# Decoding the first float64 weights through PSUM, with the rebias multiply on ScalarE

## The chip, the cores and the metric

The kernel runs on one core of a Trainium2 chip. TensorE (PE) multiplies matrices into PSUM, VectorE (DVE) and ScalarE (ACT) read PSUM and work elementwise, GpSimd (POOL) works elementwise on SBUF, and SyncE (SP) issues most DMAs. The five engines run their own instruction lists in order and wait for each other by semaphores. The metric is the device time of one execution in microseconds (us), less is better.

## The reference

The weights come as float64, everything else as float32. For each of 8 batches and 8 heads (576 tokens of 64 values), linear attention:

```python
q_s = exp(q - max(q, -1)); q_s /= sum(q_s, -1) + 1e-9
k_s = exp(k - max(k, tokens)); k_s /= sum(k_s, tokens) + 1e-9
attn = q_s @ (k_s.T @ v)
```

The heads, side by side, are x of 576 x 512 per batch. Then a token mixer with a residual, and two channel MLPs, the second after a layer norm:

```python
u = x + (relu(x.T @ w_tok1) @ w_tok2).T
y = u + relu(u @ w_ch1) @ w_ch2
out = y + relu(norm(y) * g_ln @ w2_ch1) @ w2_ch2
```

## The kernel before, in words

Products are made nearly exact in float32 by splitting each factor into a high part (rounded to TensorE's fp32r) and a low rest, and adding three products (high x high, high x low, low x high).

A weight arrives as pairs of 32-bit words. `decode` turns a chunk (up to 128 rows x 512 numbers) in a staging buffer into the high and low part in five steps:

1. rebias (L104): the upper word, read as a float32, is multiplied by 2^-112 in place;
2. shift (L107): that word is shifted left by 3 and masked, into a buffer `t`;
3. sign (L111): the sign bit is put into `t`;
4. low (L114): the top bits of the lower word are put in; the result goes back over the lower word in the staging buffer (for the weights of the second MLP it stays in `t`);
5. parts: the high part by a copy on ScalarE (L122), the low part by a subtraction on GpSimd (L123). The weights of the second MLP do this otherwise and are not in the part that is changed.

Steps 1 to 4 run on VectorE. `t` lies in SBUF, in two buffers. The staging buffers are six for the first weights (`st` two, `stages` two, `more` two).

The first weights are 30 chunks: six of the token mixer, then 24 of `w_ch1` and `w_ch2`. The class `Loads` decodes them in pairs. Its list for a pair is: both rebias steps, the parts of the pair before, the loads ahead, then both shifts, both signs, both lows. `pump(n)` issues the next n entries of the list.

The program is written out by a clock of ticks. In the first stage the attention units 0 to 7 (two heads each, batches 0 and 1; they are "early") begin four ticks apart, each with sixteen steps at set ticks, and after each tick the loop pumps four, later two, entries of the decoding. The steps of a unit that are named below: maximum of k (`kmx`, L398) and of q (`qm`, L404); transpose of `kmx` on TensorE into `pt` and its maximum `kmd` (L412); `kmd` spread out by TensorE into `pb`, copied by ScalarE into `kb` (L427); subtractions on GpSimd (L416, L431); exponentials on ScalarE (of q L441, of k into `kt` L444); sum of q (`qs`, L448) and scaling; `pk` = k x v (L463), whose sum column gives `ks` (L469); `pg` = q x w_tok1 (L486), copied into `gs` (L491); transposes of q into `pq` (L512), copied by L516; `ph` (L525), split into `hs` (L126 on ScalarE, L127 on VectorE); and twice `pu` (L540), split into `u` and `ue` (high by L122 on ScalarE, low by L123 on VectorE).

The eight PSUM banks are `acc0` to `acc3`, two `h` and two `a`. The early units take a bank for each of these products in turn from all eight (`psum(name, True)`); each product then waits until the bank's former content has been read.

After that stage the first MLP runs batch by batch (`Phase1`: L602 into `ph`, relu and split by L126 and L127, L619 into `acc`), with the rest of the 24 chunks decoded beside its first batch, and the units 8 to 31 beside the next ones. Then come the ends of the batches, the layer norm and the second MLP (`Phase2`: L732, L747).

Of the kernel before, what the change touches and what calls it, by code (L numbers as in the profile page):

```python
# [8 lines left out]
F32 = mybir.dt.float32  # L9
F32R = mybir.dt.float32r  # L10
U32 = mybir.dt.uint32
AF = mybir.ActivationFunctionType
ALU = mybir.AluOpType
# [3 lines left out]
P = 128  # L17
# [3 lines left out]
REBIAS = 2.0 ** -112  # L21
# [3 lines left out]
def kernel(  # L25
# [22 lines left out]
    nc = tc.nc  # L48
# [23 lines left out]
    main = ctx.enter_context(tc.tile_pool(name="main", bufs=1))  # L72
    ps_acc = ctx.enter_context(tc.tile_pool(name="ps_acc", bufs=1, space=PSUM))
    ps_hid = ctx.enter_context(tc.tile_pool(name="ps_hid", bufs=2, space=PSUM))
# [10 lines left out]
    def decode(st, w, hi, lo):  # L85


        rows, n = st.shape[0], st.shape[1]
        w0, w1 = st[:, :, 0], st[:, :, 1]
        wf = w1.bitcast(F32)  # L90
        t = main.tile([P, 512], U32, tag="t", bufs=2, name="t")[:rows, 0:n]

        o = t if w2p else w0
        x, vec = w(o.bitcast(F32)), nc.vector

        def parts():
            if w2p:
                vec.tensor_copy(out=hi, in_=x)  # L98
                nc.gpsimd.tensor_tensor(out=lo, in0=x, in1=hi.bitcast(F32), op=ALU.subtract)  # L99
            else:  # L100
                split(x, hi, lo, nc.gpsimd)

        return [
            lambda: vec.tensor_scalar(  # L104
                out=wf, in0=wf, scalar1=REBIAS, scalar2=None, op0=ALU.mult
            ),
            lambda: vec.tensor_scalar(  # L107
                out=t, in0=w1, scalar1=3, scalar2=0x7FFFFFF8,
                op0=ALU.logical_shift_left, op1=ALU.bitwise_and,
            ),  # L110
            lambda: vec.scalar_tensor_tensor(  # L111
                out=t, in0=w1, scalar=0x80000000, in1=t, op0=ALU.bitwise_and, op1=ALU.bitwise_or
            ),
            lambda: vec.scalar_tensor_tensor(  # L114
                out=o, in0=w0, scalar=29, in1=t,
                op0=ALU.logical_shift_right, op1=ALU.bitwise_or,
            ),
            parts,
        ]

    def split(x, hi, lo, engine):
        nc.scalar.activation(out=hi, in_=x, func=AF.Copy)  # L122
        engine.tensor_tensor(out=lo, in0=x, in1=hi.bitcast(F32), op=ALU.subtract)  # L123
# [7 lines left out]
    extra, bufs = [], []  # L131
# [9 lines left out]
    def ch1_chunk(dst, src, g, i, pool):  # L141
        def load():
            if dst is wa and (g, i) == (NF1 // 2 - 1, 0):

                extra[:] = [x for x in extra if x < 2]
            st = stage(512)
            a = src[2 * i * P:2 * (i + 1) * P, 4 * g * P:4 * (g + 1) * P]
            nc.sync.dma_start(
                out=st.rearrange("p (k f) t -> p k (f t)", k=2),
                in_=a.rearrange("(k p) f -> p k f", p=P),  # L150
            )
            return st

        def use(st):
            if i == 0:
                dst[g] = pool.tile([P, 2, KD, 2 * P], F32R, tag="w", bufs=pool_bufs[pool], name="w")
            w, kk = dst[g], slice(2 * i, 2 * i + 2)
            return decode(
                st, lambda x: x.rearrange("p (k f) -> p k f", k=2), w[:, 0, kk], w[:, 1, kk]
            )  # L160

        return load, use

    def ch2_chunk(dst, src, g, i, pool):
        def load():
            st = stage(512)
            f0 = (2 * g + i) * P
            nc.sync.dma_start(out=st.rearrange("p d t -> p (d t)"), in_=src[f0:f0 + P, :])
            return st

        def use(st):
            if i == 0:
                dst[g] = pool.tile([P, 2, 2, DM], F32R, tag="w", bufs=pool_bufs[pool], name="w")
            return decode(st, lambda x: x, dst[g][:, 0, i], dst[g][:, 1, i])

        return load, use
# [7 lines left out]
    w2p = []  # L184
# [3 lines left out]
    w1 = att.tile([P, 2, NC + 1, T], F32R, name="w1")  # L188
# [5 lines left out]
    def tok1_chunk(c0, n, rows):  # L194
        def load():
            st = stage(n * T)[:rows]
            if c0 < NC:
                src = w_tok1[0:S0].rearrange("(p c) t -> p c t", c=NC)[:, c0:c0 + n]
            else:
                src = w_tok1[S0:S].rearrange("(p c) t -> p c t", c=1)  # L200
            nc.sync.dma_start(out=st.rearrange("p (c t) w -> p c (t w)", c=n), in_=src)
            return st

        def use(st):
            return decode(
                st, lambda x: x.rearrange("p (c t) -> p c t", c=n),
                w1[:rows, 0, c0:c0 + n], w1[:rows, 1, c0:c0 + n],
            )

        return load, use  # L210
# [98 lines left out]
    rows = [P] * NC + [R]  # L309
# [51 lines left out]
    turns = [0]  # L361

    def psum(name, early=False):
        if early:
            turns[0] += 1
            i = turns[0] % 8
            if i < 4:
                return ps_acc.tile([P, 512], F32, tag=f"acc{i}", name=name)
            if i < 6:
                return ps_hid.tile([P, 512], F32, tag="h", name=name)  # L370
        return ps_att.tile([P, 512], F32, tag="a", name=name)

    class Unit:
# [34 lines left out]
        def k_top(self):  # L408
            pt = psum("pt", self.early)
            nc.tensor.transpose(out=pt[:, 0:P], in_=self.kmx, identity=ident)  # L410
            self.kmd = att.tile([P, 1], F32, tag="kmd", bufs=2, name="kmd")
            nc.vector.tensor_reduce(out=self.kmd, in_=pt[:, 0:P], axis=AX, op=ALU.max)  # L412
# [8 lines left out]
        def k_sub(self):  # L421
            pb = psum("pb", self.early)
            nc.tensor.transpose(
                out=pb[:, 0:P], in_=self.kmd.to_broadcast([P, P]), identity=ident
            )
            kb = place(self.n, "kb")
            nc.scalar.activation(  # L427
                out=kb[:, 0], in_=pb[:, 0:P].rearrange("p (h d) -> p h d", h=2), func=AF.Copy
            )
            self.kt = place(self.n, "kt")  # L430
            nc.gpsimd.tensor_tensor(  # L431
                out=self.kt, in0=self.kr.rearrange("p h c d -> p c h d"),
                in1=kb.to_broadcast([P, NC + 1, 2, D]), op=ALU.subtract,
            )
            if self.n + 3 < EARLY:
                load_qk(self.n + 3)
            elif self.n + 1 >= EARLY:
                load_qk(self.n + 1)
# [21 lines left out]
        def kv(self):  # L460
            pk = psum("pk", self.early)
            for c in range(NC + 1):
                nc.tensor.matmul(  # L463
                    out=pk[:, 0:2 * D + 2], lhsT=self.kt[:, c], rhs=vt[:, c, :],
                    start=(c == 0), stop=(c == NC),
                )
            load_v(self.n + 1)
            ks = att.tile([P, 1], F32, tag="ks", bufs=2, name="ks")
            nc.vector.tensor_scalar(  # L469
                out=ks, in0=pk[:, 2 * D:2 * D + 1], scalar1=1e-9, scalar2=None, op0=ALU.add  # L470
            )
            nc.vector.reciprocal(out=ks, in_=ks)
            for h in range(2):
                r = slice(h * D, (h + 1) * D)
                nc.vector.tensor_scalar(
                    out=self.kvn[r, r], in0=pk[r, r], scalar1=ks[r], scalar2=None, op0=ALU.mult
                )
            self.kvs = place(self.n, "kvs")
            split(self.kvn, self.kvs[:, 0], self.kvs[:, 1], nc.vector)
# [284 lines left out]
    with tc.manual_schedule():  # L764
# [5 lines left out]
        for x in spare[0:2]:  # L770
            x = x[:, 0:2 * W].rearrange("p (a h c d) -> p a h c d", a=2, h=2, d=D)
# [43 lines left out]
        for j in range(NB):  # L815
            o = Phase1(j)
            steps += [(o, f) for f in range(NF1)]
        for j in range(NB):
            o = Phase2(j)
# [21 lines left out]
        for o, f in steps:  # L841
# [32 lines left out]
            ps, n = o.L1(f, tick)  # L874
            h = main.tile([P, 2, 512], F32R, tag="h", bufs=LAG + 1, name="h")
# [42 lines left out]
```

## Time and profile before

| | us |
|---|---|
| median of three runs | 1720.69 |
| lowest, highest | 1718.91, 1722.46 |
| the profiled execution | 1719.21 |
| its span from first to last instruction | 1717.2 |
| PE, DVE, ACT, POOL busy over the span | 1654.5, 703.9, 376.8, 316.0 |

The busy shares are means over stages of different kinds. In the line of 40 slices of the profile TensorE is at 3, 6 and 8 tenths in the first three slices (43 us each) and at 9 in nearly all that follow, while VectorE is at 8 to 9 in the first three and at 2 to 4 in most others. A timeline row below gives the start, the duration, the engine, the line, the operation, what it writes and reads, and in brackets the idle time of the engine before it with what ended that.

### The profile page before, as it was taken

The numbers are of one execution on the slowest core, as the hardware profiler recorded it, in microseconds if no ns is written. First come the engines' busy times: TensorE is split into PE (matmuls) and PEld (weight loads), VectorE is DVE, ScalarE is ACT, GpSimd is POOL, SyncE is SP. The second block draws the span as 40 slices with busy tenths as digits, with TensorE's granted clock in tenths as the row PEclk, the third lists the DMA queues.
The fourth block names the chain that finished last, engine by engine and source line by source line (L and its number), as shares of the span: only waits on it lengthen the run. The fifth ranks groups of instructions, "written<-read, shape, count | busy, mean of one in ns | idle before, by whom it ended". The sixth has DMA issues, their size and how long they took to land.

```text
span 1717.2 us, 19988 instructions
## 1 busy us (share of the span) xinstructions
PE 1654.5 (96%) x8104; PEld 1383.7 (81%) x8104; DVE 703.9 (41%) x1342; ACT 376.8 (22%) x758; POOL 316.0 (18%) x213
## 2 busy tenths in 40 slices
PE   3689999999999999999999899999999999999999
PEld 3678888888888888888878688888888888888887
DVE  8987444334343444436267922131312122222211
ACT  3442232323233332321111111110111111111110
POOL 5553322223132332212113200000000000000000
PEclk9889999999999999999999999999999999999999
DMA  7442111212121211214123410101010101010010
GB/s 207 123 134 85 46 56 35 67 37 70 35 67 42 60 48 40 61 44 160 47 90 114 157 60 25 49 25 49 10 65 1 74 1 56 18 43 32 1 50 25
DMA packets 96763, 103.27 MB, mean 60 GB/s; under 512 B 60128, under 2 KB 76768, under 8 KB 93216
## 3 DMA queue, kind: packets, MB, share of 16 engines
q1 hardware_dynamic: 90272, 84.17, 16.5%
q10 hardware_dynamic: 5248, 9.44, 1.5%
q0 software_dynamic: 1152, 8.39, 1.2%
q8 instruction: 64, 1.05, 0.3%
q14 instruction: 27, 0.22, 0.0%
HBM read 81.00 MB, written 20.97 MB: 59 GB/s over the span
## 4 chain that ended last, share of the span: by engine, by line
PE 56%; DVE 3%; DMA 1%; POOL 0%; issue 0%; ACT 0%; SPq 0%; ACTq 0%; DVEq 0%
PE ph L732 22%; PE acc L747 22%; PE acc L619 5%; PE ph L602 5%; PE px L707 1%; PE pu L540 1%; DMA st<-in_moe_w_ch 0%; DVE t L111 0%; PE py L564 0%; PE pg L486 0%; POOL yT L633 0%; DVE st L671 0%; DMA y_dram<-yn 0%; DMA y<-y_dram 0%; DVE t L114 0%; DVE y L696 0%
## 5 line engine op out<-in xcount | busy, mean ns | idle before, releaser
L127 DVE SCALAR_TENSOR_TENSOR h<-ph,h 128x512 fp32r<-128x512 f32 x252 | 174.0, 691 | 685.9 <-ACT h L126 685.9
L732 PE MATMUL ph<-xT,w 128*128 128x512 f32 x1728 | 421.0, 392 | 3.5 <-DVE h L127 2.4
L747 PE MATMUL acc<-w,h 128*128 128x512 f32 x1728 | 420.0, 392 | 0.0
L732 PEld LDWEIGHTS ph<-xT,w 128*128 128x128 f32 x1728 | 322.8, 188 | 75.3 <-DVE h L127 3.2
L747 PEld LDWEIGHTS acc<-w,h 128*128 128x128 f32 x1728 | 323.0, 188 | 68.8
L126 ACT ACTIVATE h<-ph 128x512 fp32r<-128x512 f32 x252 | 150.6, 598 | 880.1 <-PE ph L732 645.7
L619 PE MATMUL acc<-h,w 128*128 128x512 f32 x1296 | 328.5, 396 | 0.0
L602 PE MATMUL ph<-u,w 128*128 128x512 f32 x1296 | 327.0, 396 | 0.0
L602 PEld LDWEIGHTS ph<-u,w 128*128 128x128 f32 x1296 | 236.5, 189 | 46.1
L619 PEld LDWEIGHTS acc<-h,w 128*128 128x128 f32 x1296 | 236.2, 188 | 45.5
L762 POOL DMA_DIRECT2D out<-y x8 | 4.4, 556 | 637.2 <-DVE y L758 637.2
L486 PE MATMUL pg<-w,qn 128*128 128x256 f32 x480 | 69.9, 299 | 5.9 <-POOL qn L123 5.7
L416 POOL TENSOR_TENSOR qt<-raw,qm 128x640 f32<-128x640 f32 x24 | 30.2, 1260 | 244.3 <-PE pt L410 208.8
L486 PEld LDWEIGHTS pg<-w,qn 128*128 128x128 f32 x480 | 67.4, 207 | 9.6 <-POOL qn L123 7.5
L99 POOL TENSOR_TENSOR w<-t,w 128x512 fp32r<-128x512 f32 x32 | 42.7, 1333 | 133.4 <-DVE w L98 127.6
L540 PE MATMUL pu<-w,hs 128*128 128x288 f32 x384 | 64.9, 306 | 2.1 <-ACT hs L126 1.8
L123 DVE TENSOR_TENSOR u<-pu,u 128x288 fp32r<-128x288 f32 x64 | 27.0, 423 | 89.2 <-ACT u L122 89.0
L540 PEld LDWEIGHTS pu<-w,hs 128*128 128x128 f32 x384 | 57.4, 198 | 2.6 <-ACT hs L126 2.0
L633 POOL TENSOR_TENSOR yT<-yT,u 128x2048 f32<-128x2048 f32 x9 | 41.8, 4649 | 67.5 <-DVE yT L630 66.3
L123 DVE TENSOR_TENSOR qT<-pq,qT 128x512 fp32r<-128x512 f32 (+1 forms) x48 | 21.8, 454 | 76.4 <-ACT qT L122 76.4
L111 DVE SCALAR_TENSOR_TENSOR t<-st,t 128x512 uint32<-128x512 uint32 x43 | 51.4, 1196 | 0.9
L431 POOL TENSOR_TENSOR kt<-raw,kb 128x640 f32<-128x640 f32 x24 | 38.3, 1597 | 53.0 <-ACT kb L427 53.0
(119 smaller groups left out, 1240.8 us busy)
## 6 DMA issues: line engine op xcount, KB each, us to landing
st<-in_moe_w_ch SPq DMA_DIRECT2D x41, 512.0 KB, 3.7
y<-y_dram SPq DMA_DIRECT2D x18, 1024.0 KB, 4.8
vt<-in_v SPq DMA_DIRECT2D x64, 128.0 KB, 2.6
y_dram<-yn ACTq DMA_DIRECT2D x32, 256.0 KB, 2.4
out<-y POOLq DMA_DIRECT2D x8, 1024.0 KB, 4.1
raw<-in_k SPq DMA_DIRECT2D x27, 256.0 KB, 2.8
raw<-in_q SPq DMA_DIRECT2D x27, 256.0 KB, 3.3
stages<-in_moe_w_ch SPq DMA_DIRECT2D x9, 512.0 KB, 4.0
```

The lines of the kernel that those rows point to most:

```text
L99: nc.gpsimd.tensor_tensor(out=lo, in0=x, in1=hi.bitcast(F32), op=ALU.subtract)
L111: lambda: vec.scalar_tensor_tensor(out=t, in0=w1, scalar=0x80000000, in1=t, op0=ALU.bitwise_and, op1=ALU.bitwise_or),
L123: engine.tensor_tensor(out=lo, in0=x, in1=hi.bitcast(F32), op=ALU.subtract)
L126: nc.scalar.activation(out=hi, in_=x, func=AF.Relu)
L127: nc.vector.scalar_tensor_tensor(out=lo, in0=x, scalar=0.0, in1=hi.bitcast(F32), op0=ALU.max, op1=ALU.subtract)
L486: nc.tensor.matmul(out=pg[:, 0:T], lhsT=self.qn[:, x, c], rhs=w1[:, y, c, :], start=(n == 0), stop=(n == len(terms) - 1),)
L540: nc.tensor.matmul(out=pu[:, 0:HN], lhsT=l, rhs=r, start=(n == 0), stop=(n == len(terms) - 1))
L602: nc.tensor.matmul(out=ps, lhsT=w[:, x, kk, fo:fo + P], rhs=u[:, y, kk], start=(n == 0), stop=(n == 3 * KD - 1),)
L619: nc.tensor.matmul(out=self.acc[dd], lhsT=w[:, x, f % 2, dd * P:(dd + 1) * P], rhs=h[:, y], start=(f == 0 and n == 0), stop=(f == self.nf ...
L633: nc.gpsimd.tensor_tensor(out=yT, in0=yT, in1=u[:, 1].bitcast(F32), op=ALU.add)
L732: nc.tensor.matmul(out=ps, lhsT=w[:, x, kk, fo:fo + P], rhs=xT[:, y, kk], start=(n == 0), stop=(n == 3 * KD - 1),)
L747: nc.tensor.matmul(out=self.acc[c], lhsT=h[:, x, c * P:(c + 1) * P], rhs=w[:, y, f % 2], start=(f == 0 and n == 0), stop=(f == self.nf - 1 ...
```

## The change

For the first 30 chunks the multiply of step 1 is issued on ScalarE as a copy with a scale. The buffer of step 2 is a PSUM bank, taken from the two `a` banks at the time of step 2, in place of `t` in SBUF; the steps 3 and 4 read it there, and step 3 writes it there. Steps 2 to 4 stay on VectorE. The early units take their banks in turn from the six others. The weights of the second MLP (`late`) are decoded as before.

```diff
-        t = main.tile([P, 512], U32, tag="t", bufs=2, name="t")[:rows, 0:n]
-        o = t if w2p else w0
-        x, vec = w(o.bitcast(F32)), nc.vector
+        vec, late = nc.vector, bool(w2p)
+        box = {}
+        if late:
+            box["t"] = main.tile([P, 512], U32, tag="t", bufs=2, name="t")[:rows, 0:n]
+
+        def rebias():
+            if late:
+                vec.tensor_scalar(out=wf, in0=wf, scalar1=REBIAS, scalar2=None, op0=ALU.mult)
+            else:
+                nc.scalar.activation(out=wf, in_=wf, func=AF.Copy, scale=REBIAS)
+
+        def shift():
+            if not late:
+                box["t"] = psum("dt").bitcast(U32)[:rows, 0:n]
+            vec.tensor_scalar(
+                out=box["t"], in0=w1, scalar1=3, scalar2=0x7FFFFFF8,
+                op0=ALU.logical_shift_left, op1=ALU.bitwise_and,
+            )
...
+        return [rebias, shift, sign, low, parts]
...
     def psum(name, early=False):
         if early:
             turns[0] += 1
-            i = turns[0] % 8
+            i = turns[0] % 6
             if i < 4:
                 return ps_acc.tile([P, 512], F32, tag=f"acc{i}", name=name)
-            if i < 6:
-                return ps_hid.tile([P, 512], F32, tag="h", name=name)
+            return ps_hid.tile([P, 512], F32, tag="h", name=name)
         return ps_att.tile([P, 512], F32, tag="a", name=name)
```

The order on TensorE, GpSimd and SyncE is the same as before. On ScalarE thirty rows are new and on VectorE the same thirty are gone. Line numbers of the changed kernel are shifted (L100 is the rebias, L106 the shift, L113 the sign, L119 the low step, L135 the high part).

ScalarE at the program's start, before: the exponential of unit 0's q (L441), the copy of `kb` (L427), the first chunk's high part (L122), the exponential of `kt` (L444).

```order
L441 ACTIVATE spare<-spare 128x640
L427 ACTIVATE spare<-pb 128x128
L122 ACTIVATE w_76<-st 128x512
L444 ACTIVATE kt<-kt 128x640
L122 ACTIVATE w_76<-stages 128x512
L122 ACTIVATE qn<-spare 128x640
```

The same place now:

```order
L453 ACTIVATE spare<-spare 128x640
L100 ACTIVATE st<-st 128x512
L100 ACTIVATE stages<-stages 128x512
L439 ACTIVATE spare<-pb 128x128
L100 ACTIVATE more<-more 64x256
L100 ACTIVATE st<-st 128x512
L135 ACTIVATE w_76<-st 128x512
L456 ACTIVATE kt<-kt 128x640
L135 ACTIVATE w_76<-stages 128x512
L135 ACTIVATE qn<-spare 128x640
```

Two rebias steps stand ahead of the copy of `kb`, and two more, of the second pair of chunks, ahead of the exponential of `kt`.

ScalarE at the end of the stage, between the parts of unit 7's `kvn` (first row) and its `hs` (last row), before:

```order
L122 ACTIVATE spare<-spare 128x128
L122 ACTIVATE u<-pu 128x288
L491 ACTIVATE gs<-pg 128x256
L516 ACTIVATE spare<-pq 128x512 x2
L122 ACTIVATE w<-more 128x512
L122 ACTIVATE w<-st 128x512
L122 ACTIVATE u<-pu 128x224
L122 ACTIVATE ue<-pu 128x64
L126 ACTIVATE hs<-ph 128x256
```

The same place now:

```order
L135 ACTIVATE spare<-spare 128x128
L100 ACTIVATE stages<-stages 128x512
L100 ACTIVATE more<-more 128x512
L135 ACTIVATE u<-pu 128x288
L503 ACTIVATE gs<-pg 128x256
L528 ACTIVATE spare<-pq 128x512 x2
L135 ACTIVATE w<-more 128x512
L135 ACTIVATE w<-st 128x512
L135 ACTIVATE u<-pu 128x224
L135 ACTIVATE ue<-pu 128x64
L139 ACTIVATE hs<-ph 128x256
```

Two rebias steps stand between the part of `kvn` and the copies of `u` and `gs`.

VectorE for the first pair of chunks, before, between unit 0's `kmd` and unit 1's `kmx`:

```order
L412 TENSOR_REDUCE kmd<-pt 128x1
L104 TENSOR_SCALAR st<-st 128x512
L104 TENSOR_SCALAR stages<-stages 128x512
L107 TENSOR_SCALAR t<-st 128x512
L448 TENSOR_REDUCE qs<-spare 128x10
L449 TENSOR_SCALAR qs<-qs 128x10
L450 RECIPROCAL qs<-qs 128x10
L107 TENSOR_SCALAR t<-stages 128x512
L111 SCALAR_TENSOR_TENSOR t<-st,t 128x512
L111 SCALAR_TENSOR_TENSOR t<-stages,t 128x512
L114 SCALAR_TENSOR_TENSOR st<-st,t 128x512
```

The same place now:

```order
L424 TENSOR_REDUCE kmd<-pt 128x1
L106 TENSOR_SCALAR dt<-st 128x512
L460 TENSOR_REDUCE qs<-spare 128x10
L461 TENSOR_SCALAR qs<-qs 128x10
L462 RECIPROCAL qs<-qs 128x10
L106 TENSOR_SCALAR dt<-stages 128x512
L113 SCALAR_TENSOR_TENSOR dt<-st,dt 128x512
L113 SCALAR_TENSOR_TENSOR dt<-stages,dt 128x512
L119 SCALAR_TENSOR_TENSOR st<-st,dt 128x512
```

The two rebias rows are gone, and `dt` in PSUM stands where `t` stood.

## Rows read from the trace of the kernel before

**Rows 1.** Windows: length, busy us (count) of PE, PEld, DVE, ACT, POOL, clock, DMA.

```profile
0.00:120.03 120.03, 72.63 (x473) 68.75 (x474) 105.06 (x199) 50.76 (x120) 70.48 (x54) 0.89 0.54 154
120.03:190.00 69.97, 69.97 (x311) 57.60 (x310) 45.24 (x71) 18.12 (x32) 21.69 (x16) 1.00 0.25 74
```

**Rows 2.** Waits to 120: who for whom, us in total, times, longest.

```profile
PE pb L423 <- DVE kmd L412: 17.2, 5, 6.2
...
DVE st L104 <- DMA st<-in_moe_w_tok: 1.9, 1, 1.9
...
DVE stages L104 <- DMA stages<-in_moe_w_tok: 1.4, 1, 1.4
```

**Rows 3.** Windows to 120.03 of DVE's lines 104, 107, 111, 114, in this order.

```profile
0.00:120.03 120.03, 9.46 (x18) 0.89 0.54 154
...
0.00:120.03 120.03, 13.33 (x18) 0.89 0.54 154
...
0.00:120.03 120.03, 18.40 (x18) 0.89 0.54 154
...
0.00:120.03 120.03, 15.37 (x16) 0.89 0.54 154
```

**Rows 4.** Instructions of lines 107 and 111 to 120.03: ns min/median/max, first and last start.

```profile
L107 DVE TENSOR_SCALAR t<-st x6: 414/485/1531, 10.8 to 107.4; 128x512 uint32<-128x512 uint32 x6
...
L111 DVE SCALAR_TENSOR_TENSOR t<-st,t x6: 673/1212/2059, 12.6 to 110.7; 128x512 uint32<-128x512 uint32 x6
```

**Rows 5.** Timeline of DVE: start, us, engine, line, operation.

```profile
12.64 1.75 DVE L111 SCALAR_TENSOR_TENSOR t<-st,t 128x512 uint32<-128x512 uint32 x1
...
97.04 0.46 DVE L123 TENSOR_TENSOR u<-pu,u 128x288 fp32r<-128x288 f32 x1
...
99.90 0.28 DVE L412 TENSOR_REDUCE kmd<-pt 128x1 f32<-128x128 f32 x1
...
109.80 0.42 DVE L127 SCALAR_TENSOR_TENSOR hs<-ph,hs 128x256 fp32r<-128x256 f32 x1
```

**Rows 6.** Timeline of POOL.

```profile
12.52 1.32 POOL L451 TENSOR_TENSOR spare<-spare,qs 128x640 f32<-128x640 f32 x1 [2.04 <-DVE qs L450]
```

**Rows 7.** Instructions of line 127, whole span: ns min/median/max, first and last start.

```profile
L127 DVE SCALAR_TENSOR_TENSOR h<-ph,h x252: 658/692/693, 124.2 to 1705.6; 128x512 fp32r<-128x512 f32 x126
```

**Rows 8.** Windows from 99.90 of DVE's lines 104, 107, 111, 114, in this order.

```profile
99.90:120.03 20.13, 2.91 (x4) 0.85 0.42 120
...
99.90:120.03 20.13, 3.56 (x4) 0.85 0.42 120
...
99.90:120.03 20.13, 3.38 (x4) 0.85 0.42 120
...
99.90:120.03 20.13, 1.97 (x3) 0.85 0.42 120
```

**Rows 9.** Timeline of ACT.

```profile
53.71 0.67 ACT L122 ACTIVATE w<-st 128x512 fp32r<-128x512 f32 x1
...
106.17 0.39 ACT L491 ACTIVATE gs<-pg 128x256 f32<-128x256 f32 x1 [0.84 <-PE pg L486]
...
108.05 0.36 ACT L122 ACTIVATE u<-pu 128x224 fp32r<-128x224 f32 x1
...
113.71 0.31 ACT L122 ACTIVATE spare<-spare 128x128 fp32r<-128x128 f32 x1 [3.16 <-DVE spare L475]
...
117.52 0.38 ACT L126 ACTIVATE hs<-ph 128x256 fp32r<-128x256 f32 x1
```

**Rows 10.** The second load into `st`, issued by SP: its row, and us to landing.

```profile
L216 SPq DMA_DIRECT2D st<-in_moe_w_tok x1: 583/583/583, 11.8 to 11.8; - x1
...
DMA to landing us min/median/max: 4.1/4.1/4.1
```

**Rows 11.** Timeline of PE.

```profile
16.97 2.53 PE L463 MATMUL pk<-vt,kt 128*128 128x130 f32 x10 [9.64 <-ACT kt L444]
...
95.41 0.27 PE L410 MATMUL pt<-ident,kmx 128*128 128x128 f32 x1
```

More of the change, by code (lines that the diff above doesn't have):

```diff
@@ L90, in decode, with sign, low @@
         wf = w1.bitcast(F32)
-        t = main.tile([P, 512], U32, tag="t", bufs=2, name="t")[:rows, 0:n]
-        o = t if w2p else w0
-        x, vec = w(o.bitcast(F32)), nc.vector
+        vec, late = nc.vector, bool(w2p)
[14 more added lines that the diff above has]
+            )
+        def sign():
+            t = box["t"]
+            vec.scalar_tensor_tensor(
+                out=t, in0=w1, scalar=0x80000000, in1=t, op0=ALU.bitwise_and, op1=ALU.bitwise_or
+            )
+        def low():
+            t = box["t"]
+            vec.scalar_tensor_tensor(
+                out=t if late else w0, in0=w0, scalar=29, in1=t,
+                op0=ALU.logical_shift_right, op1=ALU.bitwise_or,
+            )
         def parts():
-            if w2p:
+            x = w((box["t"] if late else w0).bitcast(F32))
+            if late:
                 vec.tensor_copy(out=hi, in_=x)
@@ L101, in parts @@
                 split(x, hi, lo, nc.gpsimd)
[L103 to L119, printed above, removed]
+        return [rebias, shift, sign, low, parts]
     def split(x, hi, lo, engine):
```

## The prediction

> **What bounds the kernel now.** I read the line of slices on the page first, then windows of busy time, then the waits, and last the timelines of the first 120 us, one engine at a time. The windows split the span in two. Up to 120.03 us, where the first MLP's first matmul (L602) starts, VectorE is busy 105.06 of 120.03 us, GpSimd 70.48, ScalarE 50.76, and TensorE only 72.63, at a mean granted clock of 0.89 of full speed [rows 1]. In the 70 us behind it TensorE is busy all of the 69.97 us at the full clock [rows 1], although twelve of the thirty chunks are still being decoded there. So what the change does behind 120 us is hidden by TensorE, and only the first 120 us can become shorter; what they lose moves everything behind them by the same amount.
>
> In that stage the reader is to see TensorE waiting for VectorE: five times, 17.2 us in all, for `kmd`, the small maximum that VectorE comes to late in its list [rows 2]. VectorE waited for weights only at the start, 1.9 and 1.4 us for the first two chunks [rows 2]. Its four decoding lines took 9.46, 13.33, 18.40 and 15.37 us in the stage, 56.56 us in 70 instructions, over half of what it did [rows 3].
>
> Those sums hold stalls. The same sign step (L111) takes 0.673 us at the least, 1.212 at the median and 2.059 at the most [rows 4]. The one of 1.75 us begins at 12.64 [rows 5], while GpSimd is in a subtraction or product of two SBUF tiles from 12.52 to 13.84 [rows 6]; the surplus is about GpSimd's remaining time. The relu's low part (L127), as wide but with one input in PSUM, never took over 0.693 us in the rows of its wide form [rows 7], and GpSimd worked 21.69 us beside the first of them [rows 1]. So I take the surplus as the cost of two SBUF inputs beside GpSimd.
>
> The Trainium skill says the same in "SBUF — State Buffer", section "Who interferes with whom": a VectorE instruction with two SBUF inputs contends with a GpSimd instruction that reads SBUF, one with a single SBUF input outside the two-port modes does not. The trace agrees (2.059 against 0.693 us).
>
> **The change part by part.**
>
> *Rebias.* VectorE loses 18 instructions in the stage, 9.46 us. ScalarE gains them. No row shows a rebias there; the nearest is the high part, a copy of the same width in SBUF, 0.67 us [rows 9]. I take that: 18 x 0.67 = 12.1 us on an engine with 120.03 - 50.76 = 69 us to spare [rows 1]. The bounds are 0, if every one falls in a gap of ScalarE, and 12.1 us, if all delay something that is waited for.
>
> *Shift, sign, low.* 52 instructions stay. Each now has at most one SBUF input, so the stalls go. No row shows VectorE writing PSUM. The nearest row is L127 with 0.69 us for 512 columns [rows 7]; I take it for all three steps. The bounds: 0.41, the least of the shift now [rows 4], as the lower one for the shift, 0.67 for the others; and as the upper one 1.2, the median of the stalled sign step [rows 4], as if a bank read and written by one instruction cost what the stall did. 46 of the 52 are 512 wide, 46 x 0.69 = 31.7; the six of the two small chunks I put at a half of it, 2.1. Together 33.8 in place of 47.1.
>
> The Trainium skill has a rule against this change, in "VectorE: DVE Perf Modes", section "Why PSUM operands drop a tier": with a PSUM operand an fp32 instruction on one tensor loses its double rate. The shift now takes 0.414 us undisturbed [rows 4]; by the rule it would take about the 0.69 above. The median is already 0.485 and the mean 13.33 / 18 = 0.74 us [rows 3], so by the rule the shifts keep what they cost today; without it, 16 x 0.28 = 4.4 us more would be gained.
>
> VectorE's account: 56.56 - 33.8 = 22.7 us less in the stage. From this I take three things.
>
> *The last two units.* From the last `kmd` at 99.90 to 120.03 the four lines take 11.82 us [rows 8], and 11 instructions at 0.69 would take 7.6, a share of 4.2 in the account. But there the round trip kmd - `pb` - `pg` - `gs` - `pq` - `pu` - `hs` is nearly as long as VectorE's list: `gs` starts at 106.17, as soon as `pg` is done, the copy of `u` is at 108.05 [rows 9], and VectorE's `hs` comes at 109.80 [rows 5]. After that ScalarE works almost without a gap from 113.71 to 117.52 [rows 9], and two rebias steps are put into just that stretch, 1.3 us. I leave 1.0 of the 4.2: minus 3.2.
>
> *The start.* ScalarE's list has two rebias steps, of the second pair, ahead of `kt`'s exponential. The second load into `st` is issued at 11.8 and lands 4.1 later [rows 10], at 15.9. Behind it stand that rebias, a high part and the exponential, three times about 0.67, so `pk`, which waited for `kt` until 16.97 [rows 11], starts at about 17.9: minus 0.9. The copy of `kb` waits for the second chunk too, but GpSimd has time behind it. VectorE's own 3.3 us of waiting for the first two chunks goes to ScalarE; I count no gain.
>
> *The six units between.* Here a rebias in front of `gs` or of the copies of `u` delays a round trip. With about every second unit paying one, 4 x 0.57 (0.67 less the overlap with the next) = minus 2.3.
>
> *Six banks for the early units.* With eight, the transpose `pt` of the next unit starts at 95.41 [rows 11], before VectorE has read `u`'s first half at 97.04 [rows 5]. In the rotation of six it gets just that bank and must wait to 97.5. I cost this at nothing: its result is needed for `kmd`, which stands behind that reading on VectorE, at 99.90 [rows 5], over 2 us later. If that cover were gone, `pt` and the matmuls queued behind it on TensorE (two transposes, then `pk`) would shift a unit by up to those 2 us.
>
> The sum is 22.7 - 3.2 - 0.9 - 2.3 = 16.3 us, from 1719.21, the profiled execution, to 1702.9. That execution lies 1.48 under the median of the runs; from 1720.69 it is 1704.4, my prediction.
>
> **The rivals.**
>
> *The round trip decides everywhere.* TensorE and ScalarE, not VectorE, would then set a unit's pace as soon as VectorE is a little faster, and all 18 rebias steps lie in that path: 18 x 0.57 = 10.3 in place of 2.3, a gain of 8.3, 1712.4. For it speaks that the last units show it; against it TensorE's 17.2 us of waiting for `kmd`, and that its granted clock, 0.89 on average, can only rise with shorter gaps.
>
> *The whole account is paid out*, as every deduction is hidden, the clock rises and the shift keeps 0.41: 22.7 to 27, some 1696.
>
> *PSUM as input and output is slow.* At 1.2 us for the 46 wide steps the account loses 46 x 0.51 = 23.5, and nothing is left: 1720. The change then doesn't do what it says. For it: no row shows such a write. Against it: L127 reads PSUM at the plain rate.
>
> *ScalarE is held by the weights (slower).* A rebias waits in ScalarE's list for its chunk's load, and everything behind it waits too: exponentials, `gs`, `hs`. If ScalarE came to each of the eight later pairs before its load had landed and lost a landing of 4.1 us [rows 10] each time, that is 33 us against a gain of 16.3: 1737. It decides from about 2 us a pair. Against it: after the first two chunks VectorE never waited for weights [rows 2], and ScalarE's steps stand at about the same place of the order.
>
> **How the numbers follow.** The forecast, a gain of 9 to 23 us, has 0.68 (1698 to 1712). The round trip, gains of 4 to 9, has 0.13; the whole account 0.10; slow PSUM 0.05; ScalarE held 0.04. What this measurement can tell from no change is 0.2%, 3.4 us. Of the slow-PSUM case most falls within that, with a small tail of the round trip: faster 0.90, same 0.06, slower 0.04. The range of 1696 to 1714 takes in half of the whole-account case and most of the round trip.
>
> **What would show it.** In the changed profile the first L602 should start near 104 us. The sign and low steps should stand at 0.69 us with no long ones, the shift between 0.41 and 0.69, the rebias on ScalarE near 0.67; TensorE's granted clock up to that point should be above 0.89 and its waits for `kmd` shorter. From there to the end the time should be as before. It would be wrong if the wide steps took 1 us or more, if ScalarE showed waits for weights behind the first two pairs, if `pt` waited for VectorE's `u`, or if VectorE had long gaps before 104 us and the units still came no closer together.

## The result, and the profile after

The changed kernel took 1706.12 us (median of four: 1704.91, 1705.71, 1706.52 and 7784.57) beside 1720.74 for the kernel before on the same chip. By the three ordinary executions that is a ratio of 0.9911 [0.9897, 0.9925], 15.3 us less, where 1704.4 in a range of 1696 to 1714 was predicted. The fourth, the profiled one, has TensorE at over four times its usual busy time; nothing is read from it, and the profile shown here is that of a second measurement of the same kernel (`again`): 1704.95 (1703.35 to 1706.1), 0.9902 [0.9888, 0.9915], a profiled execution of 1703.35 and a span of 1701.6.

Windows of busy time of the changed kernel, up to the first MLP's first matmul (now L614) and the 70 us behind it; columns as in [rows 1]:

```profile
0.00:104.30 104.30, 66.69 (x472) 62.77 (x473) 82.48 (x181) 60.60 (x139) 65.00 (x54) 0.95 0.61 177
104.30:174.30 70.00, 70.00 (x311) 57.60 (x310) 35.88 (x60) 24.11 (x43) 19.91 (x16) 1.00 0.23 74
```

Against [rows 1] the stage is 15.7 us shorter (120.03 to 104.30), and the span 15.6 (1717.2 to 1701.6): all of the gain lies ahead of the first MLP. VectorE is busy 22.6 us less in the stage, ScalarE 9.8 more. VectorE's idle time grew from 15.0 to 21.8 us, and by that much the stage gave less than VectorE saved.

The four decoding lines in the same stage, one window each: shift (L106), sign (L113) and low step (L119) on VectorE, then the rebias (L100), now on ScalarE. Busy us and instructions follow the length:

```profile
0.00:104.30 104.30, 11.09 (x18) 0.95 0.61 177
0.00:104.30 104.30, 10.49 (x18) 0.95 0.61 177
0.00:104.30 104.30, 9.81 (x16) 0.95 0.61 177
0.00:104.30 104.30, 11.59 (x19) 0.95 0.61 177
```

The three steps that stayed on VectorE took 47.1 us before [rows 3] and take 31.4 now. Their single durations (ns, least, median, most) and those of the rebias on ScalarE:

```profile
L106 DVE TENSOR_SCALAR dt<-st x6: 672/683/695, 9.6 to 92.2; 128x512 uint32<-128x512 uint32 x6
...
L113 DVE SCALAR_TENSOR_TENSOR dt<-st,dt x6: 677/685/696, 12.0 to 95.3; 128x512 uint32<-128x512 uint32 x6
...
L119 DVE SCALAR_TENSOR_TENSOR st<-st,dt x6: 671/682/689, 13.2 to 98.1; 128x512 uint32<-128x512 uint32 x6
...
L100 ACT ACTIVATE st<-st x7: 647/671/682, 8.9 to 103.6; 128x512 f32<-128x512 f32 x7
```

The sign step, which went from 0.673 to 2.059 us in [rows 4], now stays between 0.677 and 0.696 with PSUM as input and output. The shift lost its short form, 0.414 us in [rows 4], and takes 0.68.

The waits of the stage (engine and line waiting, releaser: us in all, times, the longest), of which the first answers to the 17.2 us in [rows 2]:

```profile
PE pb L435 <- DVE kmd L424: 4.9, 4, 2.4
...
PE pt L422 <- DVE u L136: 5.3, 3, 3.5
...
DVE ks L481 <- PE pk L475: 5.3, 4, 1.7
...
DVE dt L106 <- ACT st L100: 2.8, 1, 2.8
DVE u L136 <- ACT u L135: 2.5, 2, 2.1
```

TensorE waits 4.9 us for `kmd` in place of 17.2. It also waits for a bank (`pt`, behind VectorE's reading of `u`), and VectorE, which in the stage before never waited for TensorE and had no single wait over 1.9 us, now waits for TensorE's `pk`, for ScalarE's first rebias (in place of the first two loads) and for `u`.

### The profile page after: what moved, and what is told of

Read it like the earlier page. It is cut to its first block, busy times and chain, and to the rows that moved or that the text cites. A ratio compares the mean times of both kernels' runs of the same rounds, so it can differ in the third digit from the quotient of the medians.

```text
span 7782.8 us, 19997 instructions
## 1 busy us (share of the span) xinstructions
PE 7762.1 (100%) x8104; PEld 5239.5 (67%) x8104; DVE 668.4 (9%) x1312; ACT 402.4 (5%) x788; POOL 305.0 (4%) x213
## 4 chain that ended last, share of the span: by engine, by line
PE 100%; DMA 0%; SPq 0%; DVE 0%; ACT 0%; issue 0%
PE ph L614 22%; PE acc L631 22%; PE ph L744 19%; PE acc L759 19%; PE pu L552 6%; PE pg L498 4%; PE pk L475 3%; PE py L576 1%; PE ph L537 1%; PE pq L515 1%; PE px L719 1%; PE pq L524 0%; PE pb L435 0%; PE pt L422 0%; DMA stages<-in_moe_w_tok 0%; DMA st<-in_moe_w_tok 0%
## 5 line engine op out<-in xcount | busy, mean ns | idle before, releaser
L631 PE MATMUL acc<-h,w 128*128 128x512 f32 x1296 | 1801.8, 1718 | 0.0
L614 PE MATMUL ph<-u,w 128*128 128x512 f32 x1296 | 1799.4, 1719 | 0.0
L744 PE MATMUL ph<-xT,w 128*128 128x512 f32 x1728 | 1542.2, 1156 | 0.0
L759 PE MATMUL acc<-w,h 128*128 128x512 f32 x1728 | 1529.2, 1146 | 0.0
L614 PEld LDWEIGHTS ph<-u,w 128*128 128x128 f32 x1296 | 1158.2, 915 | 464.3 <-issue 464.3
L631 PEld LDWEIGHTS acc<-h,w 128*128 128x128 f32 x1296 | 1161.0, 917 | 455.1 <-issue 454.7
L744 PEld LDWEIGHTS ph<-xT,w 128*128 128x128 f32 x1728 | 814.5, 472 | 672.6 <-issue 669.9
L759 PEld LDWEIGHTS acc<-w,h 128*128 128x128 f32 x1728 | 800.7, 465 | 668.0 <-issue 663.0
L498 PEld LDWEIGHTS pg<-w,qn 128*128 128x128 f32 x480 | 332.9, 923 | 19.8 <-issue 19.8
L498 PE MATMUL pg<-w,qn 128*128 128x256 f32 x480 | 329.4, 1035 | 0.0
```

The lines of the kernel that those rows point to most:

```text
L498: nc.tensor.matmul(out=pg[:, 0:T], lhsT=self.qn[:, x, c], rhs=w1[:, y, c, :], start=(n == 0), stop=(n == len(terms) - 1),)
L614: nc.tensor.matmul(out=ps, lhsT=w[:, x, kk, fo:fo + P], rhs=u[:, y, kk], start=(n == 0), stop=(n == 3 * KD - 1),)
L631: nc.tensor.matmul(out=self.acc[dd], lhsT=w[:, x, f % 2, dd * P:(dd + 1) * P], rhs=h[:, y], start=(f == 0 and n == 0), stop=(f == self.nf ...
L744: nc.tensor.matmul(out=ps, lhsT=w[:, x, kk, fo:fo + P], rhs=xT[:, y, kk], start=(n == 0), stop=(n == 3 * KD - 1),)
L759: nc.tensor.matmul(out=self.acc[c], lhsT=h[:, x, c * P:(c + 1) * P], rhs=w[:, y, f % 2], start=(f == 0 and n == 0), stop=(f == self.nf - 1 ...
```

## The experiments

Twelve kernels ran in three groups, each on a chip of its own. Times are medians; each group had its own runs of the kernel before (1720.97, 1721.06, 1720.59), and each ratio is against these.

### The two parts apart, and the banks alone

`again` is the changed kernel as it stands.

> The changed kernel once more, unaltered, for a profile of an ordinary execution and a tighter ratio. VectorE's account: 1704 to 1707 us; the first L614 starts at 103 to 106 us; the shift, sign and low steps at 0.67 to 0.69 us in that stage; TensorE waits for kmd less than the 17.2 us of before. Round trip as the bound: the same total, but VectorE idle for more than 25 of the first 105 us, with its idle time ended by ScalarE or TensorE.

Measured: 1704.95, as above.

`rebias_only` moves the multiply to ScalarE and leaves `t` in SBUF and the eight banks:

```diff
+                nc.scalar.activation(out=wf, in_=wf, func=AF.Copy, scale=REBIAS)
...
-            lambda: vec.tensor_scalar(
-                out=wf, in0=wf, scalar1=REBIAS, scalar2=None, op0=ALU.mult
-            ),
+            rebias,
```

> Only the rebias goes to ScalarE; the shifted word stays in SBUF and the early units keep eight banks. VectorE's account: it loses 9.46 us of instructions in the first stage and keeps the stalls of the sign and low steps; after the same deductions (start 0.9, half of the others) a gain of 4 to 7 us, 1714 to 1717. Round trip as the bound: the rebias in ScalarE's list costs as much as it saves, a gain of 0 to 2 or a loss, 1719 to 1724.

Measured: 1720.19, 0.9992 [0.9984, 1.0001]; no change. The window of its stage, and those of its shift, sign and low steps:

```profile
0.00:119.86 119.86, 74.85 (x472) 70.68 (x473) 100.92 (x184) 60.93 (x139) 71.43 (x54) 0.87 0.55 157
```

```profile
0.00:119.86 119.86, 15.24 (x18) 0.87 0.55 157
0.00:119.86 119.86, 20.31 (x18) 0.87 0.55 157
0.00:119.86 119.86, 15.44 (x18) 0.87 0.55 157
```

VectorE lost an account of 9.46 us but is only 4.1 us less busy: the three steps that stayed take 51.0 us in place of 47.1. Of these 3.9 us, 1.5 are steps of the last pair that only now fall into the window (18 low steps for 16 before); the same 52 instructions as before take 2.4 more. One of them is the shift of the third pair. With two multiplies gone from ahead of it, it starts 1.0 us sooner beside the same subtraction on GpSimd, and ends no sooner. Before, and in `rebias_only`:

```profile
27.36 1.55 POOL L123 TENSOR_TENSOR w<-st,w 128x512 fp32r<-128x512 f32 x1 [0.32 <-ACT w L122]
28.66 0.53 DVE L107 TENSOR_SCALAR t<-stages 128x512 uint32<-128x512 uint32 x1
...
27.50 1.54 POOL L129 TENSOR_TENSOR w<-st,w 128x512 fp32r<-128x512 f32 x1 [0.30 <-ACT w L128]
27.70 1.62 DVE L113 TENSOR_SCALAR t<-stages 128x512 uint32<-128x512 uint32 x1
```

The 4.1 us that VectorE was spared became idle time (15.0 to 18.9), and the stage ends 0.17 us sooner: the last `kmd` starts 1.2 us sooner (98.67), and the stretch behind it takes 1.1 us longer (21.19 in place of 20.13).

`psum_only` is the changed kernel with the multiply back on VectorE:

```diff
-            if late:
-                vec.tensor_scalar(out=wf, in0=wf, scalar1=REBIAS, scalar2=None, op0=ALU.mult)
-            else:
-                nc.scalar.activation(out=wf, in_=wf, func=AF.Copy, scale=REBIAS)
+            vec.tensor_scalar(out=wf, in0=wf, scalar1=REBIAS, scalar2=None, op0=ALU.mult)
```

> Only the shifted word goes to PSUM (with the rotation of six banks); the rebias stays on VectorE. VectorE's account: 13.3 us less in the first stage (47.1 to 33.8), a gain of 8 to 12 us, 1709 to 1713. If the long sign and low steps were not from two SBUF inputs beside GpSimd, they stay long and the time is within 2 us of 1720.7. The rebias itself, in place in SBUF, may stall a little more or less often.

Measured: 1705.01, 0.9903 [0.9889, 0.9916]: the whole gain, better than expected. Its stage, and VectorE's wait for `pk` in it:

```profile
0.00:105.86 105.86, 67.69 (x473) 63.47 (x473) 91.23 (x198) 50.78 (x120) 65.68 (x54) 0.95 0.60 174
```

```profile
DVE ks L478 <- PE pk L472: 0.3, 1, 0.3
```

Here VectorE is 13.8 us less busy than before and the stage 14.2 us shorter: what the stalls gave back was paid out in full. The wait for `pk`, 5.3 us in the changed kernel, is 0.3. VectorE's timeline between unit 3's `kmd` and its `ks` shows why, first with the multiply on VectorE:

```profile
43.87 0.28 DVE L421 TENSOR_REDUCE kmd<-pt 128x1 f32<-128x128 f32 x1
44.06 0.42 DVE L97 TENSOR_SCALAR more<-more 128x512 f32<-128x512 f32 x1
44.40 1.78 DVE L97 TENSOR_SCALAR st<-st 128x512 f32<-128x512 f32 x1
46.10 0.15 DVE L478 TENSOR_SCALAR ks<-pk 128x1 f32<-128x1 f32 x1
```

and without it, in the changed kernel:

```profile
44.08 0.28 DVE L424 TENSOR_REDUCE kmd<-pt 128x1 f32<-128x128 f32 x1
46.05 0.16 DVE L481 TENSOR_SCALAR ks<-pk 128x1 f32<-128x1 f32 x1 [1.69 <-PE pk L475]
```

Two multiplies, one of them stalled to 1.78 us, fill a gap in which VectorE otherwise stands idle: `ks` starts at 46.10 and at 46.05.

`banks_only` is the kernel before with six banks in the rotation:

```diff
-            i = turns[0] % 8
+            i = turns[0] % 6
```

> The kernel before with only the rotation of the early units cut from eight banks to six; decoding as before. VectorE's account with the cover of kmd: nothing, within 1.5 us of 1720.7. If the wait of pt for VectorE's reading of u is on the path: up to 2 us a unit, 3 to 14 us slower, 1724 to 1735, and TensorE shows waits of pt for L123.

Measured: 1720.65, 0.9995 [0.9986, 1.0004]; no change. The wait that the prediction took to be covered appears in its stage:

```profile
PE pt L410 <- DVE u L123: 7.3, 3, 4.3
```

The units are as far apart as before: 74.23 us from unit 1's `kmd` to the last, and 74.28 before. The profiled execution (1722.21, above the median) has a stage of 122.36, with 1.2 us more ahead of unit 1's `kmd` and 1.2 more behind the last; the median shows no such loss.

### Is the bank wait of the changed kernel worth anything?

`bankmap` gives the products of the early units fixed banks, so that `pt` never takes a bank that `pu` held; `bankmap_psum` is the same with the multiply on VectorE. (Bank 4 stands for the two `h`.)

```diff
-            turns[0] += 1
-            i = turns[0] % 6
+            took[name] = took.get(name, -1) + 1
+            i = BANK[name][took[name] % len(BANK[name])]
...
+    BANK = {
+        "pt": (4,), "pb": (4,), "pk": (1,), "pg": (2,), "pq": (1, 3, 4),
+        "ph": (3,), "pu": (0, 2),
+    }
```

> The changed kernel with a fixed map of the early units' products to the six banks (pu first half alone in acc0; pk and the first pq in acc1; pg and pu second half in acc2; the second pq and ph in acc3; pt, pb and the last pq in turn in the two h), so that pt never takes the bank of pu. If the idle time that the rebias step's move left on VectorE (21.8 us against 15.0 before) comes from pt waiting for VectorE's reading of u, and pk and ks behind it: 3 to 6 us faster than the changed kernel, 1699 to 1702, and no waits of pt for VectorE's L135 family. If the round trip through TensorE and ScalarE sets the pace anyway: within 1.5 us of 1705.

> The fixed map of banks with the rebias back on VectorE, the shifted word in PSUM. If the bank wait hides the rebias step: here VectorE has little idle time, so the map gives 0 to 3 us, 1702 to 1705, and bankmap is 2 to 5 us faster than this one. Round trip as the bound: both at 1705 within 1.5 us.

Measured: 1709.94, 0.9933 [0.992, 0.9945], and 1710.27, 0.9934 [0.992, 0.9947]; both slower than the rotation. The map brought a wait of its own, unit 1's `pg` for the bank that unit 0's second `pu` still held:

```profile
PE pg L502 <- DVE ue L136: 6.6, 1, 6.6
```

Unit 3's `kmd` starts at 49.12 with the map and at 44.08 without, 5.0 later (0.5 of it ahead of unit 2's `kmd`), and the stage ends at 109.51 in place of 104.30, 5.2 later. So the map lost most of its five us in that one place. From there to the last `kmd`, where `pt` never waits for `u`, it is 1.0 us faster (41.87 in place of 42.87), and behind the last 1.2 slower (18.52 in place of 17.35). A last map with `pg` on the two `h` as well is told of below.

### Does the multiply at the start cost anything?

`start_dve` puts the multiplies of the first four chunks back on VectorE, so that `kt`'s exponential does not stand behind them on ScalarE:

```diff
-            if late:
+            if late or first[0] < 4:
+                first[0] += 1
...
+    first = [0]
```

> The changed kernel with the rebias of the first four chunks back on VectorE, so that ScalarE does not wait for the loads at the start. By the term for the start (kt's exponential 0.9 us later): 0.5 to 2 us faster than the changed kernel, 1703 to 1705. If VectorE's list at the start matters more: the same or up to 1 us slower. ScalarE waits for no load behind unit 0's exponential.

Measured: 1705.13, 0.9906 [0.9892, 0.9919]: no change against 1704.95. `kt` starts at 15.68 in place of 16.51, and the stage still ends at 105.09 in its profile, 0.8 us later than in the changed kernel's.

### What the multiply costs at all

After these runs I took the multiply to be hidden on either engine. Two kernels test that. `none` leaves it out of the first 30 chunks, with one bit less in the mask; `both` keeps it on ScalarE and adds a multiply of the same size, on a tile of its own, at its old place on VectorE.

```diff
-            else:
-                nc.scalar.activation(out=wf, in_=wf, func=AF.Copy, scale=REBIAS)
...
-                out=box["t"], in0=w1, scalar1=3, scalar2=0x7FFFFFF8,
+                out=box["t"], in0=w1, scalar1=3, scalar2=0x7FFFFFF8 if late else 0x3FFFFFF8,
```

> The changed kernel without the rebias step on any engine: the shift's mask clears the top exponent bit in its place, which gives the same number for weights under 1 in size only, as all weights here are. Theory (hidden on both engines): 1702.5 to 1705, VectorE's wait of ks for pk stays at about 5 us. Rival (a saving on VectorE cancelled by ScalarE's cost): 1696 to 1701.

```diff
                 nc.scalar.activation(out=wf, in_=wf, func=AF.Copy, scale=REBIAS)
+                d = dummy[0][:rows, 0:n]
+                vec.tensor_scalar(out=d, in0=d, scalar1=1.0, scalar2=None, op0=ALU.mult)
...
+        dummy.append(main.tile([P, 512], F32, tag="t", bufs=2, name="dummy"))
+        nc.vector.memset(dummy[0], 1.0)
```

> The changed kernel with the rebias on ScalarE and, beside it, a multiply by 1 of the same kind and width (128x512, in place, on a buffer of its own) at the rebias step's place in VectorE's list, so that both engines carry the step. Theory: the step costs nothing on either engine, since on VectorE it lies in the wait for pk in front of ks and on ScalarE in idle time: 1704 to 1706.5, with VectorE's wait of ks for pk back near 0.3 us. Rival: moving it saved VectorE several us and cost ScalarE's list as much: both costs now add up, 1708 to 1713.

Measured: `none` 1699.95 (1699.02 to 1700.43), 0.988 [0.9867, 0.9894]; `both` 1707.59 (1706.58 to 1708.49), 0.9925 [0.9913, 0.9938]. My theory fell: `none` lies in the range of the rival, and `both` between the two ranges, 1.1 us above the theory's. With the two kernels above they make a square:

| multiply on | median | ratio | unit 2's `kmd` | last `kmd` | end of the stage |
|---|---|---|---|---|---|
| neither (`none`) | 1699.95 | 0.9880 | 27.57 | 84.98 | 101.40 |
| ScalarE (changed) | 1704.95 | 0.9902 | 28.95 | 86.95 | 104.30 |
| VectorE (`psum_only`) | 1705.01 | 0.9903 | 30.66 | 88.06 | 105.86 |
| both | 1707.59 | 0.9925 | 31.25 | 89.18 | 107.85 |

By the ratios the step costs 0.0022 on ScalarE, 0.0023 on VectorE and 0.0045 on both: 3.8, 4.0 and 7.7 us (5.0, 5.1 and 7.6 by the medians, which come from different groups of runs). Each ratio is known to 0.0013, so a single cost to about 3 us, and within that the costs add. The runs of the square do not overlap: the slowest of `none` (1700.43) is faster than the fastest of either middle kernel (1703.35 and 1704.56), and the fastest of `both` (1706.58) is slower than their slowest (1706.10 and 1705.43), the last by little more than the 0.4 us by which the kernel before differs between the two groups. The profiles place the cost, one execution each. Against `none`, the multiply on VectorE costs 3.1 us up to unit 2's `kmd`, nothing in the next five units (57.40 and 57.41) and 1.4 behind the last `kmd`; on ScalarE it costs 1.4, 0.6 and 0.9. The first of these places is the least certain, as unit 0's `kmd` alone starts 1.4 us apart in `none` (7.80) and `psum_only` (6.36).

The stages of `none` and of `both`:

```profile
0.00:101.40 101.40, 66.96 (x472) 63.00 (x473) 83.12 (x180) 50.69 (x120) 65.06 (x54) 0.95 0.63 181
```

```profile
0.00:107.85 107.85, 66.69 (x472) 62.29 (x473) 92.91 (x199) 60.68 (x139) 65.25 (x54) 0.95 0.58 171
```

`none` has VectorE as busy as the changed kernel has it (83.12 and 82.48 us) and ends its stage 2.9 us sooner, so those are ScalarE's: an engine that is busy 58 per cent of the stage still has a price for 11.6 us of new work.

### Where VectorE's time counts in full

From a unit's `ks` (30.67 here) to the copies of `u` VectorE's timeline in the changed kernel is nearly without gaps:

```profile
34.01 0.81 DVE L460 TENSOR_REDUCE qs<-spare 128x10 f32<-128x640 f32 x1
34.85 1.11 DVE L461 TENSOR_SCALAR qs<-qs 128x10 f32<-128x10 f32 x1
35.99 0.22 DVE L462 RECIPROCAL qs<-qs 128x10 f32<-128x10 f32 x1
36.12 1.27 DVE L410 TENSOR_REDUCE kmx<-raw 128x128 f32<-128x640 f32 x1
37.31 0.68 DVE L106 TENSOR_SCALAR dt<-st 128x512 uint32<-128x512 uint32 x1
37.90 0.69 DVE L106 TENSOR_SCALAR dt<-stages 128x512 uint32<-128x512 uint32 x1
38.62 0.46 DVE L136 TENSOR_TENSOR u<-pu,u 128x288 fp32r<-128x288 f32 x1
...
40.91 0.38 DVE L136 TENSOR_TENSOR u<-pu,u 128x224 fp32r<-128x224 f32 x1
```

ScalarE's next work, `ue` and then `gs`, waits for the end of this list:

```profile
41.33 0.22 ACT L135 ACTIVATE ue<-pu 128x64 fp32r<-128x64 f32 x1 [5.68 <-DVE u L136]
```

One step in the list, the addition of 1e-9 to the sum of q (L461, 1.11 us here), changes nothing in float32, as each sum holds the exponential of zero. `noadd` leaves it out:

```diff
-            nc.vector.tensor_scalar(out=qs, in0=qs, scalar1=1e-9, scalar2=None, op0=ALU.add)
```

The step in the changed kernel, eight times in the stage and 5.29 us in all:

```profile
L461 DVE TENSOR_SCALAR qs<-qs x8: 173/730/1107, 11.1 to 90.1; 128x10 f32<-128x10 f32 x8
```

Its long times end with a GpSimd instruction on SBUF tiles: the one above ends at 35.96, and this row at 35.93. The same 0.03 us lies between the ends at 49.23, 69.31 and 80.09.

```profile
34.37 1.56 POOL L443 TENSOR_TENSOR spare<-spare 128x640 f32<-128x640 f32 x1
```

It was tried on the first map, then on the rotation and on a second map, with `"pg": (4,)`.

> bankmap without the addition of 1e-9 to the sum of q's exponentials, which is at least 1, so that the float32 sum is the same number. It takes away 32 short VectorE instructions, eight of them in the first stage with 4.9 us in the kernel before (up to 1.1 us each beside GpSimd). If VectorE still sets the pace once the banks are right: 2 to 5 us faster than bankmap. If TensorE and ScalarE do: under 1 us.

> The changed kernel without the addition of 1e-9 to the sum of q's exponentials (at least 1, so the float32 sum is the same). If VectorE's steps between ks and u are what the units wait for, as bankmap without the addition showed (1709.9 to 1704.1): 1699 to 1701.5. If those 5.8 us were special to that map of banks: 1703 to 1705.

> As noadd, with the fixed map of banks in which pg shares the two h with pt, pb and the last pq, so that unit 1's pg no longer waits for unit 0's ue (6.6 us in bankmap); pt doesn't take pu's bank. If pt's waits of 5.3 us in the changed kernel are on no path: within 1 us of noadd. If they are: 2 to 5 us faster than noadd.

Measured: `bankmap_noadd` 1704.13, 0.9899 [0.9886, 0.9913], against 1709.94 with the step; `noadd` 1699.51 (1698.23 to 1700.08), 0.9878 [0.9864, 0.9891]; `bankmap2_noadd` 1700.44, 0.9883 [0.9868, 0.9898]. The stage of `noadd`:

```profile
0.00:100.10 100.10, 67.29 (x473) 63.81 (x474) 76.32 (x172) 60.60 (x139) 64.83 (x54) 0.93 0.63 184
```

VectorE is 6.2 us less busy and the stage 4.2 us shorter than in the changed kernel. Most of the step's 5.29 us is paid out (4.1 us by the ratios, 5.4 by the medians, 5.8 on the first map within one group). At the place shown the step took 1.11 us, and unit 3's `kmd` follows unit 2's by 15.13 us in the changed kernel and by 13.98 in `noadd`. `noadd` is faster than the kernel before and the changed one.

The second map has neither the wait of `pt` for `u` nor the first one's wait for `pg`, and is no better than the rotation. It has a wait of its own, `ph` behind ScalarE's copy of `pq`, where `ph` in `noadd` waits 3.1 us for `gs`:

```profile
PE ph L540 <- ACT spare L531: 5.7, 4, 4.0
```

So the bank wait isn't cleared of every cost: from unit 3's `kmd` to the last, `noadd` takes 40.29 us, `bankmap_noadd` 39.12 and `bankmap2_noadd` 40.04, and both maps lose 1.0 to 1.1 us behind the last. What is shown is that no map tried here gains by it.

## Why the prediction was right, and which terms were not

The total and the mechanism were right: the stall of two-input steps beside GpSimd goes when one operand moves to PSUM, and only the stage ahead of the first MLP becomes shorter. The stall itself is wider than the prediction had it. It took the surplus for the cost of two SBUF inputs, but steps with one input stall too: the shift, between 0.414 and 1.531 us in [rows 4], and the multiply at 1.78 us in `psum_only`. Within the sum two terms were mis-sized, in opposite directions.

- *What bounds the kernel.* Right. The stage ends at 104.30, where 104 was forecast. The gain is in the stage (15.7) and not behind it.
- *Shift, sign, low: 47.1 to 33.8.* Right. They take 31.4, at 0.68 us for each wide one. PSUM as input and output runs at the plain rate, so that rival is out, and the shift went up to 0.68, the value taken.
- *VectorE's account, 22.7 less.* Right, 22.6.
- *Rebias: 9.46 us off VectorE, 0.67 each on ScalarE.* The duration was right (0.671 at the median); its worth was the term that was wrong. With `t` in SBUF the move gives nothing (`rebias_only`). With `t` in PSUM it gives 1.6 us of stage in one pair of profiles and nothing in the medians (`psum_only` 1705.01, changed 1704.95). The multiplies take 10.6 us on VectorE in `psum_only`, but about half of that falls into its wait for `pk` (5.3 us in the changed kernel, 0.3 there), and what ScalarE pays is about what VectorE saves (3.8 and 4.0 us by the square).
- *The deductions, 6.4 us.* Right in size, wrong in place. The stage gave 6.8 us less than VectorE's account. But I took 3.2 for the last two units, leaving 1.0, and the stretch behind the last `kmd` gained 2.8 (20.13 to 17.35). I took 2.3 for ScalarE's step in the units between, and by the profiles it costs 0.6 there. The start was costed at minus 0.9, and `kt` does start 0.3 later than before (16.51 and 16.20), but the stretch to unit 2's `kmd` gained 7.2 (36.11 to 28.95), and `start_dve` took nothing from the time. The deduction should have stood in one line: the 9.46 us of the rebias are not paid out. The two errors made up for each other: apart, I expected 8 to 12 us of PSUM and 4 to 7 of the move, and measured 16 and nothing. That the total came within 2 us is in part luck.
- *Six banks at nothing.* Right, by `banks_only`; the maps leave room for about 1 us in the units between. The prediction named `pt` waiting for `u` as a sign of being wrong. That wait came (5.3 us) and is no such sign: its cover, `kmd` behind `u` on VectorE, held.
- *The rivals.* The round trip does not decide everywhere: `psum_only` was paid in full and `noadd` nearly so. It does decide from `kmd` to `ks`, where VectorE now idles. The whole account was not paid. ScalarE held by the weights did not come: ScalarE's waits for chunks are in the first pairs alone, and the one that reaches VectorE is the 2.8 us for the first rebias.
- *Clock.* The granted clock was above 0.89 as forecast, 0.95 in the stage.

What stays open: why ScalarE's multiplies cost 1.4 us up to unit 2's `kmd` and 0.9 behind the last one, although moving the first four back changed nothing; and whether `none` and `noadd` together would add up, which was not run.

## What to carry to other kernels

Before an instruction is moved off the busiest engine, look for the gaps in which it stands: a step that fills a wait is worth little to remove, and one in a stretch without gaps is worth most of its time. Where an instruction stalls beside another engine, change what makes it stall (here one operand to PSUM), since taking a neighbour away can let the next one stall in its place. Test each part of a change alone, with the new place and the old place crossed: a right total can stand on two wrong terms.

## What the runs showed that was not expected

- A VectorE step that writes the bank it reads costs no more than one that only reads PSUM: 0.677 to 0.696 us for the sign step, where the low part of the relu took up to 0.693 [rows 7].
- Stalls are passed on: with 9.46 us of multiplies taken from VectorE's list, the 52 steps behind them took 2.4 us more, at the place shown by starting sooner beside the same GpSimd instruction.
- A tiny instruction can stall as a wide one does: the addition on 128x10 took 0.173 us at the least and 1.107 at the most, in one kernel and at the same step of each unit, and its long times end with GpSimd's.
